# Load order and turn order in the first ten microseconds, bn_stats spread over three iterations and a new scheduler rule, in a linear-attention plus bilinear-MLP kernel

## The chip, the cores and the metric

One core of a Trainium2 chip. The metric is device time in microseconds of one execution. The span of a profile is 1.7 us shorter than the time of the same run.

## The reference

```python
x  = A_x                                   # [1, 2048, 512] bf16
xn = layernorm(x)
# A: linear attention, 32 heads of 16, features softmax(+-q w_phi), softmax(+-k w_phi)
q, k, v = split(xn @ wqkv)                 # [512, 1536]
o = phi(q) @ (phi(k)^T v) / (phi(q) . sum(phi(k)) + 1e-6)
# B: bilinear MLP, F = 1792
h = (xn @ w_gate) * (xn @ w_up)
out = x + o @ wo + h @ w_down
```

Sixteen tiles of 128 tokens are worked through. Tiles 0 to 3 take a fast way at the start: mean and centring, then transposes on TensorE. Later tiles are turned by a transposing DMA.

## The kernel before

The program records its steps with what each reads and writes. PE's order is the program's order. A list scheduler with a small cost model decides the order on the other engines, except where a step is pinned. Each engine has its list in one fixed order: in the profile of before, DVE stood 2.20 us at a centring that waited for a DMA, and began nothing else in that time.

```python
# loads, pinned; SP and ACT are the issuing queues
load_x(0, 1)
load_x(1, 1, ACT)
load_v(SP, 0)              # v's block q: rows q*128 .. of the v weights
load_v(ACT, 1)
load_x(2, 1)
load_v(ACT, 3)
load_v(SP, 2)
load_x(3, 1)
# [cut: weights of gate and up, and so on]

# the start, pinned
warm(7)                    # 7 warm-up matmuls, then one that waits for x tile 0
warm(1, 512, [("x", 0)])
ln_mean_split(0)           # half the mean on ACT, half on DVE
ln_mean_split(1)
ln_center_split(0)         # DVE
ln_center_split(1)
x_transpose(0, 2, 0)       # 2 transposes on PE, copied out by ACT
x_transpose(0, 3, 1)
warm(1, 128)
x_transpose(1, 4, 0, DVE)  # copied out by DVE
ln_mean_split(2)
x_transpose(1, 5, 1, DVE)
warm(1, 128)
ln_center_whole(2)
# then the v products of tiles 0 and 1: blocks 0 1, block 3, tile 2's transposes, block 2
# [cut: shown in the diff]

# w_up's second moment, 14 bn_stats of low priority on DVE, in main iterations 5 and 6
if t in (5, 6):
    moments(range(7 * (t - 5), 7 * (t - 4)), last)

# late loads on SP's queue, main iteration 5
load_w(SP, wd_v, ..., "wd", 1835008)     # w_down, 1.8 MB
load_w(SP, wo_v, ..., "wo", 524288)      # w_o, 0.5 MB

# each x tile from 4 on: centring on DVE, then a turn by DMA on SP's queue
def x_next(t):
    ln_apply(t)    # DVE; its buffer is free when tile t-4 has been turned
    x_turn(t)      # transposing DMA

# a unit of gate and up: 8 matmuls of 128x512 into two PSUM banks, then
#   act: g = copy(gate bank)   dve: hT = up bank * g   ("gate" below, first priority)
```

## Time and profile before

| | before |
|---|---|
| median of three runs | 213.98 us (213.87 to 214.91) |
| profiled run | 214.63 us, span 212.9 us |
| first transposing matmul | 4.49 us |
| last matmul starts | 209.98 us |

The page of the kernel before: busy time by engine, and shares of the chain that ended last.

```profile
span 212.9 us, 4028 instructions
...
PE 208.2 (98%) x1455; PEld 125.3 (59%) x1476; DVE 167.3 (79%) x281; ACT 143.8 (68%) x350; POOL 109.9 (52%) x137
...
PE 96%; DMA 1%; DVE 1%; issue 1%
```

PE is the limit: 98% busy, and 96% of the chain. What the page counts as busy can contain idle time: from 6 to 9 us it has PE busy for 3.00 of 3.00 us, although holes of 0.10 and 0.04 us stand there. So the useful quantity is the distance from the start of one matmul to the start of the next. At full rate it is 0.216 us for 512 columns, 0.109 us for 256 and 0.056 us for 128. I call what a step takes beyond that a hole. A few matmul records are missing (1455 matmuls to 1476 weight loads) and show as a step of exactly two, as the 0.432 us before 10.81 us here; these are not counted.

The weight loads (PEld) show what a hole waited for: after the start, all waits that this trace lists for TensorE stand on them (PE itself has one, of 0.8 us, before its first matmul). In this trace they ran about 0.33 us ahead of PE: in the six waits below that left a hole, the idle time before the load is 0.32 to 0.33 us longer than the hole, as 0.42 us for a hole of 0.10 us. Here are the weight loads from 6 to 9 us of the kernel before: start, duration, line, count and, in brackets, idle time and what ended it. L474 is a transpose, L247 a product.

```profile
6.00 0.15 PEld L247 LDWEIGHTS ps<-arena 128*128 128x128 bf16 x1 [0.28 <-DVE arena L483]
6.31 0.53 PEld L247 LDWEIGHTS ps<-arena 128*128 128x128 bf16 x3 [0.15 <-issue]
6.96 0.43 PEld L474 LDWEIGHTS ps<-arena 128*128 128x128 bf16 x4
7.34 0.15 PEld L247 LDWEIGHTS ps<-arena 128*128 128x128 bf16 x2
7.92 0.55 PEld L247 LDWEIGHTS ps<-arena 128*128 128x128 bf16 x4 [0.42 <-ACT arena L228]
8.83 0.23 PEld L474 LDWEIGHTS ps<-arena 128*128 128x128 bf16 x4 [0.37 <-DVE arena L439]
```

The fifth line is tile 2's first v product, waiting for ACT's copy; the sixth is tile 3's transpose, waiting for its centring. Their holes are 0.10 and 0.04 us.

The second group of holes stands between 55 and 60 us. These weight loads waited there:

```profile
55.41 0.55 PEld L247 LDWEIGHTS ps<-arena 128*128 128x128 bf16 x4 [0.46 <-DVE arena L894]
...
57.25 0.65 PEld L247 LDWEIGHTS ps<-arena 128*128 128x128 bf16 x4 [0.21 <-ACT arena L228]
58.37 0.55 PEld L247 LDWEIGHTS ps<-arena 128*128 128x128 bf16 x4 [0.47 <-DVE arena L894]
59.26 0.55 PEld L247 LDWEIGHTS ps<-arena 128*128 128x128 bf16 x4 [0.34 <-ACT arena L228]
60.23 0.23 PEld L381 LDWEIGHTS ps<-arena 128*128 128x128 bf16 x4 [0.43 <-ACT arena L228]
```

Two of them waited for a gate on DVE (holes of 0.13 and 0.14 us), the last two for ACT (0.01 and 0.10 us); the 0.21 us is less than the loads' lead over PE and left no hole. These are DVE's instructions just before and among them. L668 is bn_stats, L894 the gate, L506 a reduction, L454 a centring.

```profile
47.62 0.69 DVE L894 TENSOR_TENSOR arena<-ps,arena 128x512 bf16<-128x512 f32 x1
48.22 0.68 DVE L668 BATCH_NORM_STATS2 arena<-arena 128x6 f32<-128x512 bf16 x1
51.11 0.41 DVE L454 TENSOR_SCALAR arena<-arena 128x512 bf16<-128x512 bf16 x1 [2.20 <-DMA arena<-arena]
51.44 0.68 DVE L894 TENSOR_TENSOR arena<-ps,arena 128x512 bf16<-128x512 f32 x1
52.04 0.41 DVE L454 TENSOR_SCALAR arena<-arena 128x512 bf16<-128x512 bf16 x1
52.36 1.28 DVE L668 BATCH_NORM_STATS2 arena<-arena 128x6 f32<-128x512 bf16 x2
53.55 1.20 DVE L506 TENSOR_REDUCE arena<-arena 128x64 f32<-128x1024 bf16 x1
54.67 0.68 DVE L894 TENSOR_TENSOR arena<-ps,arena 128x512 bf16<-128x512 f32 x1
55.27 2.46 DVE L668 BATCH_NORM_STATS2 arena<-arena 128x6 f32<-128x512 bf16 x4
57.65 0.67 DVE L894 TENSOR_TENSOR arena<-ps,arena 128x512 bf16<-128x512 f32 x1
```

### The profile page before, as it was taken

The numbers are of one execution on the slowest core, as the hardware profiler recorded it, in microseconds if no ns is written. First come the engines' busy times: TensorE is split into PE (matmuls) and PEld (weight loads), VectorE is DVE, ScalarE is ACT, GpSimd is POOL, SyncE is SP. The second block draws the span as 40 slices with busy tenths as digits, with TensorE's granted clock in tenths as the row PEclk, the third lists the DMA queues.
The fourth block names the chain that finished last, engine by engine and source line by source line (L and its number), as shares of the span: only waits on it lengthen the run. The fifth ranks groups of instructions, "written<-read, shape, count | busy, mean of one in ns | idle before, by whom it ended". The sixth has DMA issues, their size and how long they took to land.

```text
span 212.9 us, 4028 instructions
## 1 busy us (share of the span) xinstructions
PE 208.2 (98%) x1455; PEld 125.3 (59%) x1476; DVE 167.3 (79%) x281; ACT 143.8 (68%) x350; POOL 109.9 (52%) x137
## 2 busy tenths in 40 slices
PE   8999999999999999999999999999999999999995
PEld 3575444444444444444444444546888898899884
DVE  4687999985995656578699988996888898898622
ACT  5479899975789999987778977664544444432220
POOL 4031554540311355999995882004549559558540
PEclk9999999999999999999999999999999999999999
DMA  5999780899100030322721340413374646537611
GB/s 163 309 300 375 134 207 0 122 345 147 30 3 0 20 78 3 52 51 49 77 45 29 65 86 0 118 53 52 45 83 125 162 85 154 134 91 175 123 49 49
DMA packets 49251, 22.29 MB, mean 105 GB/s; under 512 B 38096, under 2 KB 47696, under 8 KB 49232
## 3 DMA queue, kind: packets, MB, share of 16 engines
q1 hardware_dynamic: 48272, 21.39, 46.0%
q10 hardware_dynamic: 960, 0.66, 1.0%
q8 instruction: 11, 0.18, 0.4%
q14 instruction: 8, 0.07, 0.2%
HBM read 11.03 MB, written 2.10 MB: 62 GB/s over the span
## 4 chain that ended last, share of the span: by engine, by line
PE 96%; DMA 1%; DVE 1%; issue 1%
PE ps L247 91%; PE ps L611 2%; PE ps L553 2%; DMA arena<-in_A_x_dram 1%; PE ps L381 1%; PE ps L474 1%; DVE arena L427 0%; DVE arena L924 0%; DVE arena L434 0%; PE ps L1001 0%
## 5 line engine op out<-in xcount | busy, mean ns | idle before, releaser
L247 PE MATMUL ps<-arena 128*128 128x512 bf16 (+2 forms) x1139 | 198.4, 329 | 1.1
L247 PEld LDWEIGHTS ps<-arena 128*128 128x128 bf16 (+1 forms) x1160 | 110.7, 98 | 73.8 <-ACT arena L228 1.2
L228 ACT ACTIVATE arena<-ps 128x512 bf16<-128x512 f32 (+3 forms) x117 | 58.6, 539 | 12.9 <-PE ps L247 7.0
L228 ACT ACTIVATE arena<-arena 128x32 f32<-128x32 f32 (+9 forms) x131 | 52.9, 423 | 11.3 <-DVE arena L506 7.2
L894 DVE TENSOR_TENSOR arena<-ps,arena 128x512 f16<-128x512 f32 (+1 forms) x56 | 38.2, 683 | 11.8 <-PE ps L247 6.1
L516 POOL TENSOR_TENSOR arena<-arena 128x1024 bf16<-128x1024 bf16 x16 | 31.8, 1995 | 26.8 <-ACT arena L228 26.8
L506 DVE TENSOR_REDUCE arena<-arena 128x64 f32<-128x1024 bf16 x32 | 38.2, 1210 | 7.6 <-ACT arena L228 7.5
L228 ACT ACTIVATE arena<-ps,arena 128x512 bf16<-128x512 f32 (+1 forms) x55 | 35.9, 672 | 10.9 <-PE ps L247 10.4
L855 POOL TENSOR_TENSOR arena<-arena 128x256 f16<-128x256 f16 x32 | 23.8, 755 | 14.3 <-DMA arena<-arena 13.2
L833 DVE TENSOR_TENSOR arena<-arena 128x896 f16<-128x896 f16 x32 | 26.0, 812 | 3.4 <-PE ps L247 3.4
L228 ACT ACTIVATE ps<-ps 128x256 f32<-128x256 f32 x24 | 8.8, 368 | 29.0 <-PE ps L247 27.0
L924 DVE SCALAR_TENSOR_TENSOR arena<-ps,arena 128x256 bf16<-128x256 f32 (+1 forms) x24 | 13.2, 565 | 8.9 <-PE ps L247 8.7
L773 POOL TENSOR_TENSOR arena<-arena 128x512 f16<-128x512 bf16 x14 | 16.3, 1175 | 5.7 <-DVE arena L894 5.2
L959 POOL TENSOR_TENSOR arena<-arena 128x512 f32<-128x512 f32 x8 | 9.5, 1190 | 17.0 <-ACT arena L228 17.0
L522 POOL TENSOR_TENSOR arena<-arena 128x512 bf16<-128x512 bf16 x16 | 17.0, 1060 | 0.8
L621 DVE TENSOR_TENSOR arena<-ps,arena 128x512 f16<-128x512 f32 x16 | 11.0, 686 | 1.3 <-ACT arena L228 0.5
L405 DVE BATCH_NORM_STATS2 arena<-arena 128x6 f32<-128x512 bf16 x16 | 10.4, 668 | 0.4 <-DMA arena<-in_A_x_dram 0.4
L520 POOL TENSOR_TENSOR arena<-arena 128x32 f32<-128x32 f32 x16 | 5.2, 326 | 10.4 <-ACT arena L228 5.8
L452 POOL TENSOR_SCALAR arena<-arena 128x1 f32<-128x1 f32 x12 | 3.2, 282 | 12.3 <-ACT arena L228 12.3
L668 DVE BATCH_NORM_STATS2 arena<-arena 128x6 f32<-128x512 bf16 x14 | 8.9, 680 | 0.0
L553 PEld LDWEIGHTS ps<-arena 128*128 128x128 bf16 x128 | 6.1, 97 | 3.5
L454 DVE TENSOR_SCALAR arena<-arena 128x512 bf16<-128x512 bf16 x12 | 5.4, 484 | 2.8 <-DMA arena<-arena 2.6
(54 smaller groups left out, 72.9 us busy)
## 6 DMA issues: line engine op xcount, KB each, us to landing
arena<-in_A_x_dram SPq DMA_DIRECT2D x8, 256.0 KB, 3.3
out_dram<-arena SPq DMA_DIRECT2D x15, 128.0 KB, 2.1
arena<-in_B_w_down_dram SPq DMA_DIRECT2D x1, 1792.0 KB, 10.1
arena<-in_A_x_dram SPq DMA_DIRECT2D x3, 512.0 KB, 4.4
arena<-arena SPq DMA_TRANSPOSE x44, 3.1
arena<-in_B_w_gate_dram SPq DMA_DIRECT2D x1, 640.0 KB, 8.7
arena<-in_B_w_up_dram SPq DMA_DIRECT2D x1, 640.0 KB, 9.9
arena<-in_B_w_gate_dram SPq DMA_DIRECT2D x1, 512.0 KB, 5.1
```

What stands on the lines that cost most here:

```text
L228: return sc.step(ACT, lambda e: e.activation(out=out_ap, in_=in_ap, func=func, scale=scale, **kw), reads, writes, 130.0 + 0.833 * n)
L247: ins = e.matmul(out_ap, lhsT=l, rhs=r, start=start and i == 0, stop=stop and i == npair - 1, **kw)
L405: dve(lambda e: e.bn_stats(stats_v[:, t, 0:6], x_tile(t)), [("x", t)], [("st", t)], 512)
L506: dve(lambda e: e.tensor_reduce(out=sm, in_=e_v, axis=AX.X, op=ALU.add), [(name, s, 0), (name, s, 1)], [("sums", sr)], 1024)
L516: pool(lambda e: e.tensor_tensor(out=e_w, in0=e_w, in1=r_w, op=ALU.mult), [(name, s, 0), (name, s, 1), ("rs", n)], [(name, s, 0), (name, s ...
L522: pool(lambda e: e.tensor_tensor(out=e_v[:, :, 1, :], in0=e_v[:, :, 1, :], in1=rat[:, :, None].to_broadcast([128, H, 16]), op=ALU.mult), [ ...
L621: dve(lambda e: e.tensor_tensor(out=o_tile(t).rearrange("p (b h f) -> p b h f", b=2, f=16), in0=nd[:, :, :, 0:16], in1=w_v[:, r].unsqueeze ...
L773: pool(lambda e, ft=ft: e.tensor_tensor(out=hH_v[:, ft, 0:512], in0=hT_v[:, ft, 0:512], in1=r2w, op=ALU.mult), [("hT", ft, 0), "r2w", ("x" ...
L833: dve(lambda e, k=k, i0=i0, i1=i1, op=op: e.tensor_tensor(out=s_block(p, k), in0=i0, in1=i1, op=op), ks + more, [s_key(p, k)] + over.get(k ...
L855: pool(lambda e, k=k, i0=i0, i1=i1, op=op: e.tensor_tensor(out=so_block(p, k), in0=i0, in1=i1, op=op), ks + [("so", p, m) for m in more], ...
L894: dve(lambda e: e.tensor_tensor(out=h_v[:, ft, sg * 512:(sg + 1) * 512], in0=bank(bu), in1=g, op=ALU.mult), [("ps", bu), ("g", s)] + ([("j ...
L924: dve(lambda e: e.scalar_tensor_tensor(out=o, in0=src, scalar=inv, in1=resid, op0=ALU.mult, op1=ALU.add), keys + [rkey, "inv"], [("ostg", ...
```

## The change

Its intent is to take the last waits out of PE's stream. Tile 2 of x is loaded ahead of v's block 0 and its mean is taken earlier. Tile 3's transposes stand behind the first half of a gate unit. The bn_stats are spread over three iterations. And the scheduler lets a first-priority step pass if it can begin within half the cost of the step that is ready.

```diff
     load_x(0, 1)
     load_x(1, 1, ACT)
+    load_x(2, 1)
+    load_v(ACT, 1)
     load_v(SP, 0)
-    load_v(ACT, 1)
-    load_x(2, 1)
     load_v(ACT, 3)
 ...
     x_transpose(0, 2, 0)
+    ln_mean_split(2)
     x_transpose(0, 3, 1)
     warm(1, 128)
     x_transpose(1, 4, 0, DVE)
-    ln_mean_split(2)
+    ln_center_whole(2)
     x_transpose(1, 5, 1, DVE)
     warm(1, 128)
-    ln_center_whole(2)
     for t in range(2):
-        v_matmul(t, t, ((0, 1),), stop=False)
-    for t in range(2):
-        v_matmul(t, t, ((3,),), start=False, stop=False)
+        v_matmul(t, t, ((1,), (0,)), stop=False)
     x_transpose(2, 6, 0)
     x_transpose(2, 4, 1, DVE)
     for t in range(2):
-        v_matmul(t, t, ((2,),), start=False)
+        v_matmul(t, t, ((3,), (2,)), start=False)
 ...
     v_matmul(2, 2)
+    g0a()
     x_transpose(3, 7, 0)
-    x_transpose(3, 6, 1, DVE)
+    x_transpose(3, 3, 1, DVE)
 ...
-    g0a()
     u0a()
+    g1a()
     v_matmul(3, 3)
     v_keep(3, 3)
-    g1a()
     u1a()
 ...
-        if t in (5, 6):
-            moments(range(7 * (t - 5), 7 * (t - 4)), last)
+        if 5 <= t < 8:
+            moments(range(5 * (t - 5), min(NF, 5 * (t - 4))), last)
 ...
-                soon = min(begin(p) for p in lst) + 100.0
-                cand = min((p for p in lst if begin(p) <= soon), key=...)
+                head = min(lst, key=lambda p: (begin(p), steps[p[1]].prio, p[1]))
+                soon = begin(head) + max(100.0, 0.5 * costs[head[1]][0] if costs[head[1]] else 0.0)
+                cand = min((p for p in lst if begin(p) <= (soon if steps[p[1]].prio == 0 else begin(head) + 100.0)), key=...)
```

More of the change, by code (lines that the diff above doesn't have):

```diff
@@ L1282, in begin @@
                     return max(t, lock_free) if costs[p[1]] and costs[p[1]][1] else t
-                soon = min(begin(p) for p in lst) + 100.0
-                cand = min((p for p in lst if begin(p) <= soon), key=lambda p: (steps[p[1]].prio, begin(p), p[1]))
+                head = min(lst, key=lambda p: (begin(p), steps[p[1]].prio, p[1]))
+                soon = begin(head) + max(100.0, 0.5 * costs[head[1]][0] if costs[head[1]] else 0.0)
+                cand = min((p for p in lst if begin(p) <= (soon if steps[p[1]].prio == 0 else begin(head) + 100.0)),
+                           key=lambda p: (steps[p[1]].prio, begin(p), p[1]))
                 key = (begin(cand), cand[1])
```

## The prediction

> **What bounds the kernel.** TensorE (PE) issue, almost without a hole. The page: PE 98% busy (208.2 of 212.9 us); the chain that ended last is 96% PE. [...] I read start-to-start distances in the PE timeline: a 128x512 matmul every 0.216 us, a 128x256 every 0.109 us, nearly throughout from 4.49 us (first transpose) to 209.98 us (last matmul). The change neither removes nor adds a matmul; it can only win PE holes:
>
> - 0 to 4.49 us: x tile 0 lands (3.38), mean, centring. Untouched.
> - 4.5 to 6.0 us: half rate (128-column matmuls 0.107 apart, 512-column 0.427).
> - 6 to 9 us: 0.10 us before tile 2's first v matmul (7.61, waits for ACT's copy of its transpose) and 0.04 us before tile 3's transpose (8.58, waits for its centring).
> - 55 to 60 us: holes of 0.13, 0.01, 0.14 and 0.10 us, 0.38 together: gates (DVE, 0.68 us) stand behind runs of bn_stats over w_up (four in a row, 0.6 us apart, from 55.27).
> - Tail, 209.98 to 212.9 us (last eviction and store): same order in both kernels.
>
> **What the change does.**
> 1. x tile 2 goes before v's block 0 on SP's queue. Landings before: x2 5.67, block 0 4.27, block 1 4.48. After, I expect x2 near 4.3 and block 0 near 5.6; the v products begin with block 1 and need block 0 at 6.0, so no new wait. Tile 2's mean runs at 5.2 rather than 5.7, its centring ends near 6.3 rather than 6.72, and its transposes go after four v matmuls, not six (near 6.75 rather than 7.17). Four v matmuls (0.86 us) then cover ACT's copy: the 0.10 us hole closes.
> 2. The first gate half-unit (4 x 0.109 us) goes before tile 3's transposes; its weights landed at 7.33. The 0.04 us hole closes.
> 3. The fourteen bn_stats of w_up are spread 5/5/4 over three iterations instead of 7/7, and the list scheduler lets a nearly ready gate go ahead of a longer low-priority step. In the new DVE order one or two bn_stats stand between gates, once three (four before). I expect most of the 0.38 us back. But the rule reorders DVE from 20 us to the end; I allow 0.1 us of new holes. The last bn_stats moves nearer the norm product, which had about 5 us of slack (copy at 65.0, reduction at 71.0).
>
> **Sum.** 0.14 + 0.35 - 0.1 = about 0.4 us of 214, 0.2%: 213.6 us, range 212.9 to 214.5. The width is run noise: the three runs before differ by 1.0 us, [...] the moment of full rate varies. This one trace shows it near 6.0 us. 2% would need 4.3 us, more than all holes.
>
> **What would show it.** First tile-2 transpose near 6.75 us; no 0.3 us step at its v product; 128x512 matmuls between 50 and 65 us 0.216 us apart throughout; PE's last matmul 0.4 to 0.5 us earlier; tail as before.
>
> **What would make it wrong.** Block 0 landing after 6.0 us (a hole early on); a gate delayed by a DVE step that waits for a transposing DMA (several centrings now stand in a row near 37 us); the norm product stalling PE because bn_stats end later; full rate arriving at another moment.

That the moment varies is shown by the table of the experiments: 3.65 to 6.68 us.

## The result and the profile after

| | before | after |
|---|---|---|
| median (6 runs each, same rounds) | 214.31 us (213.87 to 214.91) | 213.75 us (213.60 to 214.54) |
| ratio | | 0.9983 (0.9959 to 1.0006) |
| profiled run's span | 212.9 us | 212.6 us |
| first transposing matmul | 4.49 us | 4.78 us |
| holes, 6.5 to 13 us | 0.16 us | none |
| holes, 45 to 65 us | 0.43 us | none |
| last matmul starts | 209.98 us | 209.70 us |

The ratio is the mean time of the one kernel's fast runs over that of the other's in the same rounds, so it is not quite the ratio of the medians. It means 0.36 us of 214 (0.0017 x 214), and its interval holds 1. The holes add every step more than 8 ns over its nominal length, so the 0.43 us here contains the 0.38 us of the prediction.

The page after:

```profile
span 212.6 us, 4047 instructions
...
PE 208.8 (98%) x1476; PEld 125.6 (59%) x1476; DVE 165.8 (78%) x281; ACT 144.6 (68%) x350; POOL 108.8 (51%) x137
...
PE 97%; DMA 1%; DVE 1%; issue 0%
```

The larger PE count is no more work: the trace before lacks 21 matmul records. The weight loads of the first 10 us after:

```profile
6.30 0.15 PEld L247 LDWEIGHTS ps<-arena 128*128 128x128 bf16 x1 [0.28 <-DVE arena L483]
6.60 0.10 PEld L247 LDWEIGHTS ps<-arena 128*128 128x128 bf16 x1 [0.16 <-issue]
6.82 0.42 PEld L474 LDWEIGHTS ps<-arena 128*128 128x128 bf16 x4
7.20 2.10 PEld L247 LDWEIGHTS ps<-arena 128*128 128x128 bf16 x12
9.31 0.32 PEld L474 LDWEIGHTS ps<-arena 128*128 128x128 bf16 x4
```

From 6.82 us on no load waits: both waits of before are gone. Tile 2's transposes now stand at the third line, behind four v products; tile 3's, at the fifth, come behind the first gate half-unit. And DVE near 50 us after:

```profile
49.28 0.67 DVE L894 TENSOR_TENSOR arena<-ps,arena 128x512 bf16<-128x512 f32 x1
49.87 1.28 DVE L668 BATCH_NORM_STATS2 arena<-arena 128x6 f32<-128x512 bf16 x2
51.90 0.69 DVE L894 TENSOR_TENSOR arena<-ps,arena 128x512 bf16<-128x512 f32 x1 [0.76 <-PE ps L247]
52.51 1.21 DVE L506 TENSOR_REDUCE arena<-arena 128x64 f32<-128x1024 bf16 x1
53.63 0.82 DVE L454 TENSOR_SCALAR arena<-arena 128x512 bf16<-128x512 bf16 x2
```

No long run of bn_stats, and no wait for a DMA either: the two centrings stand behind a gate and a reduction, and DVE is early enough to wait for PE (0.76 us) instead of the reverse. The turn that the first centring needs landed even later than before, at 53.45 us (51.01 before). Both explanations fit this trace.

The spans differ by only 0.30 us although 0.58 us of holes are gone, because x tile 0 landed 0.30 us later in the profile after (3.68 against 3.38 us), and the first transpose came 0.29 us later with it. The new load order is not what made it late: tile 0 landed at 3.39 to 3.68 us in the five traces with that order and at 3.34 to 3.67 us in the nine with the old one. Of the prediction's other signs, the first transpose of tile 2 stood at 7.03 us (6.74 without the late start, 6.75 predicted), the tail was as before (2.91 against 2.92 us), and the last matmul came only 0.29 us earlier, not 0.4 to 0.5. The sum closes: in every trace but one, the time from the first transpose to the last matmul is 204.08 us plus its excess over nominal distances, to 0.02 us once holes that look like a missing record are counted. The excess is what the experiments compare.

### The profile page after: what moved, and what is told of

It is laid out like the page before. It is cut to its first block, busy times and chain, and to the rows that moved or that the text cites. A ratio compares the mean times of both kernels' runs of the same rounds, so it can differ in the third digit from the quotient of the medians.

```text
span 212.6 us, 4047 instructions
## 1 busy us (share of the span) xinstructions
PE 208.8 (98%) x1476; PEld 125.6 (59%) x1476; DVE 165.8 (78%) x281; ACT 144.6 (68%) x350; POOL 108.8 (51%) x137
## 4 chain that ended last, share of the span: by engine, by line
PE 97%; DMA 1%; DVE 1%; issue 0%
PE ps L247 91%; PE ps L553 2%; PE ps L611 2%; DMA arena<-in_A_x_dram 1%; PE ps L381 1%; PE ps L474 1%; DVE arena L427 0%; DVE arena L924 0%; DVE arena L434 0%; PE ps L1001 0%
## 5 line engine op out<-in xcount | busy, mean ns | idle before, releaser
L228 ACT ACTIVATE arena<-ps 128x512 bf16<-128x512 f32 (+3 forms) x117 | 59.3, 538 | 17.9 <-PE ps L247 12.4
L228 ACT ACTIVATE arena<-arena 128x32 f32<-128x32 f32 (+8 forms) x131 | 52.4, 424 | 6.0 <-DVE arena L894 3.0
L516 POOL TENSOR_TENSOR arena<-arena 128x1024 bf16<-128x1024 bf16 x16 | 31.0, 1934 | 38.0 <-ACT arena L228 38.0
L855 POOL TENSOR_TENSOR arena<-arena 128x256 f16<-128x256 f16 x32 | 24.3, 768 | 13.0 <-DMA arena<-arena 11.7
L833 DVE TENSOR_TENSOR arena<-arena 128x896 f16<-128x896 f16 x32 | 23.7, 749 | 3.2 <-PE ps L247 3.1
L520 POOL TENSOR_TENSOR arena<-arena 128x32 f32<-128x32 f32 x16 | 4.2, 266 | 9.5 <-ACT arena L228 9.5
L553 PEld LDWEIGHTS ps<-arena 128*128 128x128 bf16 x128 | 6.0, 97 | 3.5
L802 DVE TENSOR_TENSOR arena<-arena 128x1792 f16<-128x1792 f16 (+1 forms) x8 | 7.0, 903 | 0.0
L611 PEld LDWEIGHTS ps<-arena 128*128 128x128 bf16 x128 | 6.2, 97 | 1.2
```

What stands on the lines that cost most here:

```text
L228: return sc.step(ACT, lambda e: e.activation(out=out_ap, in_=in_ap, func=func, scale=scale, **kw), reads, writes, 130.0 + 0.833 * n)
L516: pool(lambda e: e.tensor_tensor(out=e_w, in0=e_w, in1=r_w, op=ALU.mult), [(name, s, 0), (name, s, 1), ("rs", n)], [(name, s, 0), (name, s ...
L611: ins = e.matmul(bank(b0 + c // 4, (c % 4) * CW, CW), lhsT=ph[:, c, :], rhs=kvz_v[:, c, :], start=True, stop=True)
L833: dve(lambda e, k=k, i0=i0, i1=i1, op=op: e.tensor_tensor(out=s_block(p, k), in0=i0, in1=i1, op=op), ks + more, [s_key(p, k)] + over.get(k ...
L855: pool(lambda e, k=k, i0=i0, i1=i1, op=op: e.tensor_tensor(out=so_block(p, k), in0=i0, in1=i1, op=op), ks + [("so", p, m) for m in more], ...
```

## The experiments

Two theories for the holes near 57 us: A, runs of bn_stats between gates (the prediction's); B, the centring that waits for a late DMA turn and holds up DVE. For the first 10 us: closed waits, against a rival in which the load order alone does it, or costs something.

Excess in the traces, in us. "Full rate" is where the trace's clock record begins; where there is none, it is read from the step lengths. "Third load" is the landing of what SP's queue issues third: tile 2 with the old load order, block 0 with the new one.

| kernel | full rate from | excess, first transpose to 6.5 us | third load lands | holes 6.5 to 13 | holes 45 to 65 | DVE waits for the turn |
|---|---|---|---|---|---|---|
| before | 6.17 | 0.82 | 5.67 | 0.16 | 0.43 | 2.20 |
| before_look | 3.72 | 0.38 | 5.36 | 0.25 | 0 | 0.70 |
| mid_only | 4.60 | 0.39 | 5.32 | 0.34 | 0 | 0.30 |
| spread_only | 6.20 | 0.84 | 5.55 | 0.16 | 0 | 1.19 |
| rule_only | 4.53 | 1.29 | 6.95 | 0.48 | 0 | 0.54 |
| first_stats | 4.80 | 0.39 | 5.75 | 0.38 | 0.02 | 0 |
| late_wd | 6.68 | 0.95 | 6.22 | 0.16 | 0 | 0 |
| after | about 6.5 | 0.82 | 5.72 | 0 | 0 | 0 |
| again | 4.17 | 0.38 | 5.55 | 0 | 0 | 0 |
| head_only | 3.75 | 0.46 | 5.72 | 0 | 0 | 1.42 |
| old_loads | 5.41 | 0.39 | 5.29 | 0 | 0 | 0 |
| old_loads_2 | 6.20 | 0.69 | 5.41 | 0 | 0 | 0 |
| gap_fill | about 6.6 | 1.16 | 6.43 | 0 | 0 | 0 |
| turn3_first | 3.65, lost at 7.06 | 1.68 | 6.91 | see there | 0 | 0 |

The 0.38 us in the third column is time left open among the first transposes, which follow DVE's centring (four steps, 1.11 us in before). In turn3_first, at full rate, the ten 128-column matmuls from the first transpose on took 0.94 us (4.50 to 5.44) where ten full-rate steps of 0.056 are 0.56. In before, at half rate, they took 1.09 us (4.49 to 5.58), and ten steps of 0.107 are 1.07: half rate filled nearly all of that time, so the late full rate added only 0.44 us (0.82 - 0.38).

The kernels again, head_only, mid_only and old_loads ran in one set of rounds; before had there a median of 214.29 us (214.02 to 215.17, 11 runs).

**again** (no edit).

> The changed kernel once more, unaltered. Measure: from the start of the first transposing matmul to the start of the last matmul in the trace (before 205.49 us, after 204.91 us). If the gain is closed PE holes, this comes out at 204.9 +- 0.1 again, with no 128x512 step over 0.25 us after 7 us, and 0.2 to 0.3% by the clock. If x tile 0 landed late (3.68 against 3.38 us) because tile 2 now stands second on its queue, it lands near 3.7 again; if that was noise, it lands anywhere from 3.3 to 3.7.

Measured: 214.19 us (213.69 to 214.81), ratio 0.9987 (0.9962 to 1.0012). First transpose to last matmul took 204.47 us, not 204.9, but only because full rate came at 4.17 us: the excess fell by 0.44 us. Holes: none, as before. x tile 0 landed at 3.46 us. My chosen yardstick was bad, since it contains the moment of full rate; from here on I compare holes. The gain is too small for the clock: two sets of rounds gave 0.9983 and 0.9987, each interval holding 1.

**head_only**: loads and first 12 us of the change, with

```diff
-        if 5 <= t < 8:
-            moments(range(5 * (t - 5), min(NF, 5 * (t - 4))), last)
+        if t in (5, 6):
+            moments(range(7 * (t - 5), 7 * (t - 4)), last)
 # and the scheduler rule of before
```

> Loads and order of the first 12 us as in the changed kernel, bn_stats and scheduler rule as before. Closed holes: the two holes at 7.6 and 8.6 us (0.14 us) go, holes near 50 to 60 us stay (0.2 to 0.5 us; the order there shifts a little), so 205.3 +- 0.15 us from first transpose to last matmul. Rival, the early loads carry the whole gain: 204.9 us. x tile 0: near 3.7 us if tile 2 behind it slows it, 3.3 to 3.7 if noise.

Measured: 214.49 us (213.63 to 214.95), ratio 0.9994 (0.9968 to 1.0020). The head's holes are gone, as expected. The holes near 57 us are gone as well, which I had not expected: bn_stats stood 7/7 and the rule was the old one. But the scheduler's order on DVE had shifted: a gate now stood ahead of the waiting centring, DVE waited 1.42 us there, not 2.20, and the longest run of bn_stats was three, not four. So my expectation missed, but the run does not decide between the theories.

**mid_only**: the reverse, bn_stats and rule of the change with loads and first 12 us of before.

> bn_stats spread and scheduler rule as in the changed kernel, loads and first 12 us as before. Closed holes: the head keeps its 0.14 us, the holes of 50 to 60 us (0.38 us) go, so 205.1 +- 0.1 us from first transpose to last matmul, more than half of the gain. Rival, the early loads carry the gain: 205.5 us. x tile 0 near 3.4 us if tile 2 behind it is what slows it.

Measured: 214.02 us (213.88 to 214.15), ratio 0.9978 (0.9959 to 0.9997). No holes near 57 us. The head's holes stayed and were 0.34 us, not 0.14: with full rate from 4.60 us PE came to tile 2's transposes sooner (their weight loads began at 6.55 us, 6.96 in before), while the load that tile 3's centring needs landed no sooner, at 7.49 us (7.41 in before, with full rate from 6.17 us). This is the only interval that leaves out 1; with one trace I cannot tell what part of it the closed holes have and what part the moment of full rate.

**old_loads** and **old_loads_2**: the change with one edit undone.

```diff
-    load_x(2, 1)
-    load_v(ACT, 1)
     load_v(SP, 0)
+    load_v(ACT, 1)
+    load_x(2, 1)
```

> The changed kernel with the load order of before (tile 2 behind v's block 0), all compute in the new order. If the new order needs the early tile, DVE waits for tile 2 until about 5.7 us ahead of its copy of tile 1's transpose, PE gets a hole of 0.1 to 0.4 us between 6 and 7.5 us, and the time from first transpose to last matmul is 205.0 to 205.3 us. Rival, the load order is idle and the compute order does it all: 204.9 us. x tile 0 near 3.4 us if tile 2 behind it is what slows it.

> The changed kernel with the load order of before, a second profile. The first had no hole, but tile 2 landed at 5.29 us there. If it lands at 5.6 us or later, DVE waits for it ahead of tile 1's copy and PE gets a hole of 0.1 to 0.4 us near 6 to 7 us; if the load order is idle, none up to a landing of 6 us.

Measured: old_loads 214.45 us over six runs (213.75 to 215.62 fast, and one at 217.14 us with a clock of 0.992, counted slow), ratio 1.0031 (0.9987 to 1.0075); old_loads_2 214.24 us, one run. Neither trace has a hole after 6.5 us, with tile 2 at 5.29 and 5.41 us. Where the third load is this early, the new compute order closes the holes without the new load order. What happened in the run of 217.14 us was not profiled.

The next four ran together; before had a median of 214.43 us (213.88 to 215.23, 7 runs).

**late_wd**: the order of before on every engine except SP's queue, where two turns pass the loads of w_down and w_o.

```diff
     by_eng, order = _order(sc)
+    sp = by_eng[SP]
+    at = next(i for i, st in enumerate(sp) if st.lane == ("dma", 28))
+    loads, turns = sp[at:at + 2], sp[at + 2:at + 4]
+    sp[at:at + 4] = turns + loads      # [cut: sequence numbers, and the same move in `order`]
```

> The kernel before with one change of SP's queue: the loads of w_down and w_o (2.3 MB) are issued behind the two turns of x that stood behind them; every other engine keeps its exact order, the run of four bn_stats included. Theory A (the prediction's): the run of four bn_stats delays the gates, so the holes of 55 to 60 us (0.38 us) stay. Theory B: DVE's idle time of 2.20 us at 48.9 us, in a centring that waits for a turn which lands behind those loads (51.01 us), makes the backlog; then the turn lands by about 46 us, that idle time goes, and the holes shrink to under 0.1 us although the four bn_stats still stand in a row.

Measured: 214.16 us (213.85 to 214.56, 4 runs), ratio 0.9982 (0.9949 to 1.0016). DVE in its trace:

```profile
48.59 0.68 DVE L668 BATCH_NORM_STATS2 arena<-arena 128x6 f32<-128x512 bf16 x1
49.19 0.39 DVE L454 TENSOR_SCALAR arena<-arena 128x512 bf16<-128x512 bf16 x1
49.50 0.68 DVE L894 TENSOR_TENSOR arena<-ps,arena 128x512 bf16<-128x512 f32 x1
...
52.74 0.68 DVE L894 TENSOR_TENSOR arena<-ps,arena 128x512 bf16<-128x512 f32 x1
53.34 2.46 DVE L668 BATCH_NORM_STATS2 arena<-arena 128x6 f32<-128x512 bf16 x4
55.72 0.67 DVE L894 TENSOR_TENSOR arena<-ps,arena 128x512 bf16<-128x512 f32 x1
```

The four bn_stats still stand in a row, for the same 2.46 us. The wait is gone, since the turn landed at 42.98 us instead of 51.01. In the other 13 traces, where the loads stand ahead, the first turn behind them landed 0.48 to 0.50 us after w_o did; its landing follows the loads. There is no hole from 45 to 65 us. That is as theory B has it and not as A has it, although one trace without holes decides less than I thought: see before_look.

**spread_only** and **rule_only**: the kernel before with one of the two edits of the middle.

> The kernel before with bn_stats spread 5/5/4 and the old scheduler rule; the longest run between gates is three. Theory A: holes of 45 to 65 us under 0.1 us. Theory B: the order still has the centring that waits for the turn ahead of a gate, so DVE idles about 2 us near 49 us and holes of 0.1 to 0.4 us stay. Head holes as before: 0.14 us, or about 0.3 us if the full clock comes before 5 us.

> The kernel before with the new scheduler rule and bn_stats in 7/7; the longest run is three. Theory A: holes of 45 to 65 us under 0.1 us. Theory B: as well, but because gates now pass the centring that waits for the turn: DVE idle there under 1 us. Head holes as before, 0.14 to 0.33 us by the clock's phase.

Measured: 214.23 us and 215.11 us, one run each. No holes near 57 us in either. In spread_only DVE did wait, 1.19 us, and that was not enough to make a hole, so my expectation of theory B was too strict. In rule_only it waited 0.54 us. Since before_look, below, has no holes with neither edit, these two runs do not show that either edit closed them. The slow time of rule_only is its start: v's block 3 landed at 7.17 us (5.85 before), and PE stood 0.90 us for it.

**first_stats**: bn_stats at first priority, two runs of seven.

```diff
     keys = [("wu", s) for s in range(len(SLICES))]
-        sc.prio = 2
+        sc.prio = 0
```

> The kernel before with bn_stats raised to first priority, so that two runs of seven (4.2 us each) stand between gates. Theory A: holes of 1 to 3 us in all in 45 to 65 us, several times the 0.38 us of before. Theory B alone: no more than the 0.2 to 0.5 us that the wait for the turn gives.

Measured: 214.14 us, one run. From DVE's timeline:

```profile
52.78 0.40 DVE L454 TENSOR_SCALAR arena<-arena 128x512 bf16<-128x512 bf16 x1
53.10 4.24 DVE L668 BATCH_NORM_STATS2 arena<-arena 128x6 f32<-128x512 bf16 x7
57.27 1.27 DVE L894 TENSOR_TENSOR arena<-ps,arena 128x512 bf16<-128x512 f32 x2
```

Seven bn_stats hold DVE for 4.24 us between two gates, and the holes of the whole stretch come to 0.02 us. Theory A expected 1 to 3 us. A run of bn_stats alone does not make the holes: in this order the gates have that much slack when DVE is not already late.

The last four ran together; before had a median of 214.24 us (213.96 to 215.30, 11 runs).

**before_look** (no edit; the kernel before again).

> The kernel before, unaltered, a second profile. If the holes of 55 to 60 us come from the turn that lands late (51.01 us in the first profile), they follow that landing: with a landing before 50.3 us and DVE idle under 1.4 us, as the trace with bn_stats spread had, holes under 0.1 us; with a landing near 51 us, about 0.4 us again. If they belong to the order of instructions alone, about 0.38 us whatever the landing. Head holes 0.14 us, or about 0.3 us if the full clock comes before 5 us.

Measured: 213.88 us, one run. The same instructions in the same order as the first profile, and no hole from 45 to 65 us. The line that differs:

```profile
49.27 0.41 DVE L454 TENSOR_SCALAR arena<-arena 128x512 bf16<-128x512 bf16 x1 [0.70 <-DMA arena<-arena]
...
53.44 2.46 DVE L668 BATCH_NORM_STATS2 arena<-arena 128x6 f32<-128x512 bf16 x4
```

The turn landed at 49.18 us, DVE waited 0.70 us in place of 2.20, and the run of four harmed nothing. So the 0.43 us of the first profile belong to that execution's late landing, not to every execution of the kernel before. It is the only one of the fourteen traces with such holes, so a trace without them is no proof that its edit removed them.

**turn3_first**: the change with tile 3's transposes ahead of the half-unit.

```diff
     v_matmul(2, 2)
-    g0a()
     x_transpose(3, 7, 0)
     x_transpose(3, 3, 1, DVE)
+    g0a()
```

> The changed kernel with tile 3's transposes ahead of the first gate half-unit, as before. Tile 3 lands near 7.4 us and is centred near 8.6 us. A hole before its transpose returns: about 0.04 us if the full clock comes near 6.2 us, 0.2 us or more if it comes before 5 us. If the half-unit in front did nothing, no hole over 0.02 us.

Measured: 216.60 us, one run, clock 0.992. It does not answer its question, because everything in it came late. Its weight loads:

```profile
5.39 0.10 PEld L247 LDWEIGHTS ps<-arena 128*128 128x128 bf16 x1
6.95 0.11 PEld L247 LDWEIGHTS ps<-arena 128*128 128x128 bf16 x2 [1.47 <-DMA arena<-in_A_wqkv_dram]
7.29 0.15 PEld L247 LDWEIGHTS ps<-arena 128*128 128x128 bf16 x1 [0.23 <-issue]
```

Block 0 of v landed at 6.91 us, and PE stood 1.30 us for it. Then the clock fell: its record grants full rate from 3.65 us for 3.41 us, half rate for the next 3.41 us, and full rate from 10.47 us on. The table of stretches (length, busy time by engine, granted clock third from last) shows it:

```profile
4.50:9.10 4.60, 3.47 (x20) 1.71 (x21) 2.10 (x10) 1.55 (x6) 0.00 (x0) 0.78 1.00 319
```

An estimate of the cost from these numbers: 1.30 us of standing still and 1.7 us for 3.41 us at half rate (3.41 / 2), 3 us together. Against "again", the excess to 6.5 us is 1.30 us larger (1.68 - 0.38), and first transpose to last matmul is 3.0 us longer (207.46 against 204.47). From 36 us on the kernel is within 0.02 us of all others but the first profile of before. In the 3.41 us before the fall PE was idle for 0.41 and 1.13 us and busy for 1.87. In rule_only, with its hole of 0.90 us and PE busy for 2.61 us of the first 3.41 us at full rate (4.53 to 7.94 us), the clock stayed. One trace of each does not show what made the clock fall.

**gap_fill**: a try at a faster version.

```diff
     warm(1, 512, [("x", 0)])
+    warm(3, 128)
```

> The changed kernel with three more 128-column warm-up matmuls in the gap between the last warm-up matmul (ends near 4.2 us) and the first transpose (4.5 to 4.8 us). If that gap holds back the full clock, it now comes at 4.2 us in every run and all times fall to the lowest seen, 213.6 us, spread under 0.3 us. If the moment of the full clock is free of what the kernel does, it scatters between 4.2 and 6.7 us as before, times 213.6 to 214.8 us, same median as the changed kernel within 0.3 us.

Measured: 214.71 us (214.16 to 214.84, 6 runs), ratio 1.0011 (0.9989 to 1.0032). Full rate came at about 6.6 us although the gap before the first transpose was shorter (its weight load waited 0.23 us, 0.95 in the profile after), so in this execution the gap was not what held it back. The profiled run also had block 0 late:

```profile
6.48 0.13 PEld L247 LDWEIGHTS ps<-arena 128*128 128x128 bf16 x2 [0.66 <-DMA arena<-in_A_wqkv_dram]
```

with a hole of 0.50 us. This kernel differs from the change by three warm-up matmuls alone, and its six runs do not show the change's gain. No version is clear of noise from the changed kernel; in the rounds that they share, mid_only's median (214.02 us) lies even below that of again (214.19 us).

## Why the prediction was right or wrong

The time was right: 213.6 us predicted, 213.75 us measured, inside the range, and a ratio that means 0.36 us where 0.4 us was forecast. That they agree so closely is partly luck: the interval holds 1, the largest term (0.35 us) was priced from an execution that proved exceptional, and the head's term (0.14 us) was too small. The account was right on PE, on what closes the head's holes and on the noise, wrong on the holes near 57 us, and too sure of block 0.

*PE issues without a hole, so only holes can be won: right.* PE reads 98% busy before and after, while the step distances show 0.59 us of holes before and 0.01 us after; the busy time could not have shown the difference.

*The head's two holes close: right in mechanism, its size was off.* The term 0.14 us was read from one trace with full rate from 6.17 us. In the three traces of the old order with full rate after 6 us it is 0.16 us, in three with full rate before 5 us it is 0.25 to 0.38 us (before_look, mid_only, first_stats), and in rule_only, with its late loads, 0.48 us. All traces of the change's order with its loads in time have none. In these traces this part of the change was worth more with an earlier full rate; the load for tile 3 did not come earlier with it (7.49 us in mid_only, 7.41 in before).

*"gates (DVE, 0.68 us) stand behind runs of bn_stats over w_up": wrong.* This is the step that failed. Late_wd kept the run of four and lost the holes; first_stats made runs of seven and got 0.02 us; before_look has the same order and no holes. What made the difference was DVE standing 2.20 us in a centring whose buffer waits for a DMA turn. The turn was issued at 42.51 us, behind 2.4 MB of w_down and w_o, and landed at 51.01, 8.5 us later, where the median turn takes 3.1 us; the same turn landed at 42.98 us once it was issued ahead of those loads. The reduction behind the centring (53.55 us) had its input from ACT at 51.63 us and so ran 1.92 us late; in before_look it ran 0.43 us after its input, in late_wd 0.12. The delay then passed through ACT, whose next step needs DVE's reduction and which holds gate copies behind it; this is ACT in the kernel before:

```profile
54.79 0.26 ACT L228 ACTIVATE arena<-arena 128x64 f32<-128x64 f32 x1 [3.17 <-DVE arena L506]
```

The first hole (0.13 us, before the matmul at 55.41 us) waited for the gate at 54.67, which stands ahead of the run of four; that alone might have warned me. In the second (0.14 us, before 58.38) the run had a share: its gate, at 57.65 us, had its copy from ACT at 57.21 and then stood behind the last bn_stats. But in before_look and late_wd the same run held the same gate 0.45 us past its copy, and no hole came of it; so as far as these traces show, the run cost something only on top of the late turn. In the order after, a gate and a reduction stand ahead of that centring, and it starts 0.18 us after its turn has landed (53.63 against 53.45 us), so DVE does not stand still; the margin is small, and by my estimate a turn later by more than this would hold up the gate behind it; no trace has that. Whether the wait alone, with no bn_stats behind it, would make holes was not tried. The value of this part is also not the 0.38 us of one trace: the second profile of before had none, so its mean is less, by how much is open.

*"so no new wait" for block 0: right in the profile after, not in general.* The third load of SP's queue (128 KB) landed between 5.29 and 6.95 us over fourteen traces, whichever load it was, and this spread decided more than the change did (holes of 0.50, 0.90 and 1.30 us, against a gain of 0.36 us). With the new load order that load is v's block 0, which PE needs for its second v product, at 5.7 to 6.3 us. Of the five traces with the new load order, three had it by 5.72 us (head_only with a hole of 0.07 us), and two, gap_fill and turn3_first, had holes of 0.50 and 1.30 us. The prediction named this as what would make it wrong, but gave it no weight. With the old order of before, block 0 lands at 4.3 to 4.7 us and PE has work until block 3 is needed; its one trace with a very late third load (rule_only) lost 0.90 us, and kept its clock. So the change removes small holes that every trace of the old compute order has, and adds exposure to a late load in some. In the two sets of rounds of the changed kernel itself no run lost 3 us (twelve runs, at most 214.81 us), but smaller losses cannot be told from the times: gap_fill's profiled run, with its hole of 0.50 us, took 214.59 us.

*Run noise: right.* Full rate began anywhere from 3.65 to 6.68 us for kernels with the same warm-up. Once begun, it lasts 208.21 us in eleven of the twelve clock records; in turn3_first it was lost after 3.41 us and came back 3.41 us later. What sets the moment is not shown by these traces. Before and before_look differ by 0.44 us of excess for this alone, which is more than the whole change.

What stays open: the mean gain by the clock, as all intervals of the full change hold 1; why both traces of the new load order in the last set had late loads, while the two of the old order in that set had not; what tile 3's turn behind the half-unit is worth by itself; and what sets the moment of full rate and made it end in turn3_first.

## What to carry to other kernels

Follow a late step back along its engine's queue to the last time that engine stood still: a run of work just ahead of it is only a suspect, and an in-order engine blocked by a DMA may have lost the time several microseconds earlier (here DVE stood still until 51.11 us, and the first hole ended at 55.41). Profile the same kernel twice before pricing a hole, because holes of this size moved with one landing (0.43 us with the turn at 51.01 us, none with it at 49.18) or with the moment of full rate (0.16 us in the head with 6.17 us, 0.25 with 3.72). With PE 98% busy, the risk that remained here is a load that lands late in the first microseconds (the third at 5.29 to 6.95 us), and the wait may not be its whole cost: after 1.30 us in turn3_first PE ran at half rate for 3.41 us, after 0.90 us in rule_only it did not.
